# 64 short idle products for four wide ones in the head, and the last output tile's products in two halves, in a packed-attention and mixture-of-experts kernel

## The chip, the cores and the metric

The kernel runs on one core of a Trainium2 chip. The metric is the device time of one execution in microseconds (us), as the median of several runs. The engines are TensorE (PE in the profile, PEld for its weight loads), VectorE (DVE), ScalarE (ACT), GpSimd (POOL) and SyncE (SP, which issues most transfers). TensorE writes its results to PSUM, which has eight banks of 512 float32 columns on 128 partitions.

## What is computed

```python
def _attn_ref(q, k, v, p):          # q, k, v: 8 batches, 8 heads, 576 rows, 64 wide; p: 32 rows
    p_packed = sm_attn(p, k, v)     # sm_attn: softmax(scale * qq @ kk.T) @ vv
    out = sm_attn(q, p_packed, p_packed)
    return out
...
def _moe_ref(x, w_gate, w_output_gate, w1, w2):   # x: 4608 rows of 512; 8 experts, 1024 wide
    logits = x @ w_gate
    e_idx = np.argmax(logits, axis=1)
    ...
    for e in range(E):
        mask = e_idx == e
        h = np.maximum(x[mask] @ w1[e], 0.0)
        ye = h @ w2[e]
        out[mask] = gate_w[mask, None] * eom[mask, e, None] * ye
```

Two softmax attentions follow each other, the first of which packs each batch to 32 rows. Each row of the result then goes through one expert of a mixture of experts, and is scaled by its two gates.

## The kernel before, in words

The eight batches run one after another as a pipeline. Three pieces of work belong to a batch. `encode` computes the packed rows from p, k and v; `route` makes the second attention's weights and the gates; `weights` and `values_up` fetch the expert most of the batch's rows want, and fold its w1 with the packed values into G. `ffn(b)` then forms the hidden layer as products of the attention weights with G (line 674, eight chunks of 128 features), and the output as products of the hidden layer with w2. Both operands of these products are split into a high and a low part, so each chunk takes three products (`three`, line 79). The hidden layer is made for columns 0 to 255 and then for 256 to 575 of a batch (`halves`, line 603). Rows whose expert is another one are computed by `leftover`, for the first seven batches beside batch 7's work.

The order of the work is written by hand (line 939): a string START for the head, and a table PLANS for each batch, which says after which step of `ffn` which step of the other pieces is issued. Each engine's queue follows that order. PSUM banks come from two groups of four (`bank`, line 68, tags "a" and "f").

**The head.** Until TensorE has ffn work, `keep_warm(i)` (line 113) issues products of zeros whose results nobody reads. The number of them at place i is `CFG["warm"][i]`. Place 8 is called once, in batch 1's `packed_whole` (line 317), between the scores of the first and of the second half of k: at this place stand four products of 512 columns in bf16. The loop over `CFG["short"]` (line 117) belongs to place 0 and issues none, as the number is 0.

**The last tile.** `product_out` (line 701) makes one tile of 128 output rows by 512 columns: eight chunks by three products, all accumulated in one bank, with a yield after every second chunk at which the plan may put other work. The last batch takes its tiles in the order `last=(4, 2, 3)`: the remainder of 64 rows first (lines 729 to 741), then tile 2, then tile 3, which ends the kernel:

```python
            if (b, t_) == (B - 1, CFG["last"][-1]):
                rows = out[b * S + t_ * P:b * S + (t_ + 1) * P]
                right = sb.tile([P, DM // 2], F32, tag="ob", name="right", bufs=CFG["ob"])
                nc.vector.tensor_scalar_mul(ob[:, :DM // 2], ps[:, :DM // 2], sc)
                nc.scalar.activation(right, ps[:, DM // 2:], AF.Copy, scale=sc)
                nc.sync.dma_start(rows[:, :DM // 2], ob[:, :DM // 2])
                nc.sync.dma_start(rows[:, DM // 2:], right)
```

VectorE scales its left half and ScalarE its right, both from the same bank, and SyncE stores each half by a transfer of its own.

Of the kernel before, what the change touches and what calls it, by code (L numbers as in the profile page):

```python
# [10 lines left out]
F32 = mybir.dt.float32  # L11
# [3 lines left out]
AF = mybir.ActivationFunctionType  # L15
# [3 lines left out]

P = 128  # L20
BANK = 512
CFG = dict(raw=6, rq=2, pa=4, w1=2, wst=4, w2=6, a1T=2, at=2, row=2, ht=4, ob=4, up="faaf", last=(4, 2, 3), short=0, warm=(4, 1, 0, 2, 1, 1, 2, 2, 4),
           pool=("w1.0", "w1.1", "w1.2", "w1.3", "w2.0", "w2.1", "w2.2", "w2.3", "w3.3", "w4.3", "w5.3", "w6.3", "w7.3",
                 "al0.0.0"))

# [16 lines left out]
def tile_packed_attn_then_moe(ctx, tc, qT, kT, v, pT, w_go, w1, w2, kp, out):  # L42


    nc = tc.nc
    B, _, _, NPAIR, HS = qT.shape
    NG, S = v.shape[1], 2 * HS
    NP = pT.shape[3]
    E, DM, DF = w1.shape[0], out.shape[1], BANK * w1.shape[1] // 2
# [3 lines left out]
    TF = S // P  # L53
# [4 lines left out]
    FC = DF // P  # L58
# [3 lines left out]
    sb = ctx.enter_context(tc.tile_pool(name="sb", bufs=1))  # L62
    WIDE, EVEN = dict(align_bytes=512), dict(align_bytes=64)
    pool = ctx.enter_context(tc.tile_pool(name="ps", bufs=8, space=PSUM))

    NA = CFG["pa"]

    def bank(name, tag="a"):
        return pool.tile([P, BANK], F32, tag=tag, name=name, bufs=NA if tag == "a" else 8 - NA)
# [9 lines left out]
    def three(a, b):  # L79

        return [(a[i], b[j]) for i in range(len(a)) for j in range(len(b)) if i + j < 2]
# [31 lines left out]
    def keep_warm(i):  # L113

        ps = bank("warm", "a" if i == 5 else "f")
        if i == 0:
            for _ in range(CFG["short"]):
                nc.tensor.matmul(ps[:MQ, :MQ], idle[:, :MQ], idle[:, :MQ], start=True, stop=True)
        for _ in range(CFG["warm"][i]):
            if i == 1:  # L120
                for n in range(1):
                    nc.tensor.matmul(ps[:, n * P:(n + 1) * P], blank, blank, start=True, stop=True)
            else:
                nc.tensor.matmul(ps.rearrange("p (a n) -> p a n", a=2), idle[:, :P], wide_idle, start=True, stop=True)

    keep_warm(0)
    first = const.tile([P, 1], F32, name="first")
    ones = const.tile([P, P], F32R, name="ones")
# [14 lines left out]
    no_row = float(2 * B * S)  # L143
    key_i = sb.tile([P, B * T * Q * E], I32, tag="hT", name="key_i", bufs=CFG["ht"], **WIDE)
    nc.gpsimd.iota(key_i, pattern=[[1, B * T * Q * E]], base=int(big_id), channel_multiplier=0)
# [11 lines left out]
    row = const.tile([P, B, T], F32, name="row")  # L157
# [16 lines left out]
    def eng(what, *at):  # L174
        return nc.gpsimd if what + ".".join(map(str, at)) in CFG["pool"] else nc.vector

# [7 lines left out]
    def fetch(x):  # L184
# [5 lines left out]
        tag = "rq" if x == "q" else "raw"  # L190
        bufs = CFG[tag]
        if x == "v":
# [40 lines left out]
    def packed_by_parts(b, pt, nm2, sm, rs, ppc):  # L233
# [5 lines left out]
        for i, n in enumerate(PARTS):  # L239
            if i:  # L240
                keep_warm(5)
            ps = [bank("ps_s1", "f")[:, :n] for _ in range(NG)]
            by_head(ps, pt, pairs("k", b, i))
            s1.append(ps)
# [64 lines left out]
    def packed_whole(b, pt, nm2, sm, rs, ppc):  # L309
# [3 lines left out]
        if b == 1:  # L313
            for g in range(NG):
                nc.scalar.copy(a1[:, g, 0], s1[0][g])
            s1[0] = [a1[:, g, 0] for g in range(NG)]
            keep_warm(8)
# [329 lines left out]
    def ffn(b):  # L647
        ah, al = A.pop(b)
        for (t0, t1) in halves:
# [4 lines left out]
            for fc in range(FC):  # L654
# [29 lines left out]
                if not (b == c0 == fc == 0):  # L684
                    yield
            outs = [product_out(b, t_, c0, hs) for t_ in (CFG["last"] if last else range(t0, t1))]
            if b == 0 and not last:
                yield from chain.from_iterable(zip(*outs))
# [3 lines left out]
    keep = []  # L692

    def store():

        while keep:
            b, t_, ob, ps, sc = keep.pop(0)
            nc.scalar.activation(ob, ob if b < 2 and t_ < 2 else ps, AF.Copy, scale=sc)  # L698
            nc.sync.dma_start(out[b * S + t_ * P:b * S + (t_ + 1) * P], ob)

    def product_out(b, t_, c0, hs):
        w2s = W[b][1]
        r = min(P, S - t_ * P)
        ps = bank("ps_o", "f")
        c = t_ * P - c0
        ob = sb.tile([P, DM], F32, tag="ob", name="ob", bufs=CFG["ob"])
        sc = scm_all[:r, b, t_:t_ + 1]
        if t_ < TF:
            lo = 640 - 2 * P + c
            for fc in range(FC):  # L710
                for i, (a, m) in enumerate(three((hs[fc][:, c:c + P], hs[fc][:, lo:lo + P]), w2s[fc])):
                    nc.tensor.matmul(ps, a, m, start=fc == i == 0, stop=fc == FC - 1 and i == 2)  # L712
                if fc % 2 and (fc < FC - 1):
                    yield
            if (b, t_) == (B - 1, CFG["last"][-1]):
                rows = out[b * S + t_ * P:b * S + (t_ + 1) * P]
                right = sb.tile([P, DM // 2], F32, tag="ob", name="right", bufs=CFG["ob"])
                nc.vector.tensor_scalar_mul(ob[:, :DM // 2], ps[:, :DM // 2], sc)
                nc.scalar.activation(right, ps[:, DM // 2:], AF.Copy, scale=sc)
                nc.sync.dma_start(rows[:, :DM // 2], ob[:, :DM // 2])  # L720
                nc.sync.dma_start(rows[:, DM // 2:], right)
            else:
                keep.append((b, t_, ob, ps, sc))
                if b > 1 or t_ > 1:
                    store()
                else:
                    nc.scalar.copy(ob, ps)
        else:
            seq = []
            for fc in range(FC):  # L730
                wh, wl = w2s[fc]
                seq += [(hs[fc][:, c:c + 2 * r], w) for w in (wh, wl)]
            for i, (a, m) in enumerate(seq):
                nc.tensor.matmul(ps, a, m, start=i == 0, stop=i == len(seq) - 1)  # L734
                if i % 6 == 5:
                    yield
            low = sb.tile([r, DM], F32, tag="ob", name="low", bufs=CFG["ob"])
            nc.scalar.copy(low, ps[r:2 * r])
            nc.vector.tensor_tensor(ob[:r], ps[:r], low, ALU.add)
            nc.vector.tensor_scalar_mul(ob[:r], ob[:r], sc)  # L740
            nc.sync.dma_start(out[b * S + SF:(b + 1) * S], ob[:r])
        yield
# [201 lines left out]
    for b in range(B):  # L944
        plan = {}
        for x in PLANS[b].split():
            i, what = x.split(":")
# [71 lines left out]
```

## Time and profile before

| | us |
|---|---|
| median of 3 runs | 397.39 (396.75 to 397.51) |
| the profiled execution, its own time | 397.62 |
| its span, first to last instruction | 396.0 |
| TensorE busy | 386.6 (98%) |
| VectorE, ScalarE, GpSimd busy | 280.9, 182.4, 38.2 |

The profile is of one execution, whose own time stands beside its span; 1.6 us lie around the span. A product's time in it is its latency from start to end. Products overlap in the array, so a row that merges n of them lasts n - 1 times their distance plus one latency. The chain of waits is followed back from the last instruction, and gives at each step what the step waited for.

### The profile page before, as it was taken

How to read it: one execution, taken by the hardware profiler on the slowest of the kernel's cores; microseconds unless marked ns; L12 is line 12 of the kernel's file. 1: busy time of each engine (PE TensorE's matmuls, PEld its weight loads, DVE VectorE, ACT ScalarE, POOL GpSimd, SP SyncE). 2: the span in 40 equal slices, each digit the busy share in tenths (PEclk: the TensorE clock that was granted, in tenths of full speed). 3: DMA queues.
4: the chain of work that ended last, by engine and by line, in shares of the span. 5: the costliest groups of instructions: out<-in, count | busy, mean ns of one | idle time of the engine just before them, and what ended most of it. 6: DMA issues, size and time to landing. Idle time of an engine off the chain costs nothing.

```text
span 396.0 us, 9464 instructions
## 1 busy us (share of the span) xinstructions
PE 386.6 (98%) x3631; PEld 313.6 (79%) x3631; DVE 280.9 (71%) x798; ACT 182.4 (46%) x407; POOL 38.2 (10%) x40
## 2 busy tenths in 40 slices
PE   6899999999999999999999999999999999999995
PEld 2478886879779888787979888788887889798984
DVE  3789699588965967478755886659774796848820
ACT  4375437724645354533816237442645345441401
POOL 3100003410053000200002000020002000020010
PEclk9999999999999999999999999999999999999999
DMA  8999269918961399205990099602951059105911
GB/s 294 362 377 409 86 199 412 376 41 293 409 233 38 111 361 410 88 28 195 398 374 31 11 304 409 250 28 99 362 216 36 28 177 366 44 27 166 311 30 53
DMA packets 36541, 83.59 MB, mean 211 GB/s; under 512 B 3598, under 2 KB 16144, under 8 KB 36496
## 3 DMA queue, kind: packets, MB, share of 16 engines
q1 hardware_dynamic: 36032, 81.74, 56.4%
q10 hardware_dynamic: 432, 1.25, 0.8%
q8 instruction: 29, 0.48, 0.5%
q14 instruction: 16, 0.13, 0.1%
q0 software_dynamic: 32, 0.00, 0.0%
HBM read 67.76 MB, written 15.27 MB: 210 GB/s over the span
## 4 chain that ended last, share of the span: by engine, by line
PE 92%; DMA 4%; DVE 1%; issue 1%; SPq 1%; ACT 1%; POOL 0%; DVEq 0%
PE ps_o L712 44%; PE ps_h L85 26%; PE ps_o L734 7%; PE ps_G L92 4%; DMA w<-in_w_dram 3%; PE ps_s L92 2%; PE ps_pp L92 2%; PE ps_s2T L92 2%; PE ps_a1T L340 2%; PE ps_lg L92 1%; DMA kp<-in_kp_dram 1%; PE ps_h L662 1%; PE ps_lo L840 0%; PE ps_lh L840 0%; PE ps_ppT L375 0%
## 5 line engine op out<-in xcount | busy, mean ns | idle before, releaser
L712 PE MATMUL ps_o<-w2h,hT 128*128 128x512 f32 x512 | 165.3, 395 | 0.0
L712 PEld LDWEIGHTS ps_o<-w2h,hT 128*128 128x128 f32 x512 | 96.3, 188 | 23.1 <-issue 1.3
L712 PE MATMUL ps_o<-w2l,hT 128*128 128x512 f32 x256 | 99.9, 390 | 0.0
L681 DVE SCALAR_TENSOR_TENSOR hT<-ps_h,hT 128x256 fp32r<-128x256 f32 x192 | 60.6, 350 | 49.7 <-ACT hT L678 48.8
L85 PE MATMUL ps_h<-ah,Gh 128*128 128x320 f32 (+1 forms) x252 | 76.5, 303 | 0.0
L85 PE MATMUL ps_h<-ah,Gl 128*128 128x320 f32 (+1 forms) x252 | 74.6, 296 | 0.0
L85 PE MATMUL ps_h<-al,Gh 128*128 128x320 f32 (+1 forms) x252 | 74.5, 296 | 0.0
L678 ACT ACTIVATE hT<-ps_h 128x320 fp32r<-128x320 f32 (+1 forms) x128 | 51.4, 414 | 40.9 <-PE ps_h L85 38.7
L597 POOL TENSOR_TENSOR w2l<-wst,w2h 128x1024 fp32r<-128x1024 f32 x13 | 31.8, 2445 | 297.4 <-ACT w2h L594 268.3
L712 PEld LDWEIGHTS ps_o<-w2l,hT 128*128 128x128 f32 x256 | 48.1, 188 | 9.1
L85 PEld LDWEIGHTS ps_h<-ah,Gh 128*128 128x128 f32 x252 | 47.8, 190 | 3.4 <-ACT ah L486 0.8
L85 PEld LDWEIGHTS ps_h<-al,Gh 128*128 128x128 f32 x252 | 47.8, 190 | 0.4
L85 PEld LDWEIGHTS ps_h<-ah,Gl 128*128 128x128 f32 x252 | 47.8, 190 | 0.0
L594 ACT CAST w2h<-wst 128x1024 fp32r<-128x1024 f32 (+1 forms) x33 | 33.5, 1056 | 1.4 <-DMA wst<-in_w_dram 0.7
L698 ACT ACTIVATE ob<-ps_o,scm_all 128x512 f32<-128x512 f32 x27 | 18.6, 687 | 32.6 <-PE ps_o L712 27.3
L597 DVE TENSOR_TENSOR w2l<-wst,w2h 128x1024 fp32r<-128x1024 f32 (+1 forms) x20 | 23.3, 1167 | 5.5 <-ACT w2h L594 5.3
L466 ACT ACTIVATE s<-s 128x576 f32<-128x576 f32 (+2 forms) x18 | 11.4, 633 | 34.2 <-DVE s L463 34.2
L77 DVE TENSOR_TENSOR Gl<-ps_G,Gh 128x512 fp32r<-128x512 f32 x28 | 17.4, 681 | 12.9 <-ACT Gh L76 12.9
L734 PE MATMUL ps_o<-w2h,hT 128*128 128x512 f32 x64 | 25.7, 401 | 0.0
L734 PE MATMUL ps_o<-w2l,hT 128*128 128x512 f32 x64 | 25.1, 392 | 0.0
L486 ACT CAST ah<-a2T 128x576 fp32r<-128x576 f32 (+2 forms) x17 | 10.7, 639 | 26.5 <-DVE a2T L478 26.5
L92 PE MATMUL ps_G<-w,ppT 64*32 64x512 f32 (+1 forms) x288 | 16.5, 549 | 0.6 <-DMA w<-in_w_dram 0.6
(215 smaller groups left out, 425.6 us busy)
## 6 DMA issues: line engine op xcount, KB each, us to landing
w<-in_w_dram SPq DMA_DIRECT2D x36, 512.0 KB, 5.6
wst<-in_w_dram SPq DMA_DIRECT2D x36, 512.0 KB, 8.7
vt<-in_v_dram SPq DMA_DIRECT2D x15, 640.0 KB, 8.9
k<-in_kT_dram SPq DMA_DIRECT2D x14, 576.0 KB, 10.1
q<-in_qT_dram SPq DMA_DIRECT2D x14, 576.0 KB, 10.3
out_dram<-ob SPq DMA_DIRECT2D x31, 256.0 KB, 4.1
a_d<-a2T SPq DMA_DIRECT2D x16, 320.0 KB, 8.0
q<-in_qT_dram SPq DMA_DIRECT2D x4, 288.0 KB, 6.1
```

The source lines that it names most:

```text
L77: (lo_eng or nc.vector).tensor_tensor(lo, src, f(hi), ALU.subtract)
L85: res = nc.tensor.matmul(dst, a, m, start=j == 0, stop=j == len(seq) - 1)
L92: res = nc.tensor.matmul(dst, a, m, start=j == 0, stop=j == len(seqs[0]) - 1)
L466: nc.scalar.activation(sf[g], sf[g], AF.Exp, scale=QK)
L486: nc.scalar.copy(ah[:, g, ts], a2T[:, g, ts])
L594: nc.scalar.copy(h, x)
L597: eng("w", b, j).tensor_tensor(l, x, f(h), ALU.subtract)
L678: nc.scalar.activation(hT[:, :n], ps, AF.Relu)
L681: nc.vector.scalar_tensor_tensor(hT[:, d0:d0 + s1 - s0], ps[:, s0:s1], 0.0, f(hT[:, s0:s1]), op0=ALU.max, op1=ALU.subtract)
L698: nc.scalar.activation(ob, ob if b < 2 and t_ < 2 else ps, AF.Copy, scale=sc)
L712: nc.tensor.matmul(ps, a, m, start=fc == i == 0, stop=fc == FC - 1 and i == 2)
L734: nc.tensor.matmul(ps, a, m, start=i == 0, stop=i == len(seq) - 1)
```

## The change

Place 8 of the idle products gets none of the wide ones (the last number of `warm` goes from 4 to 0). The loop of short products moves from place 0 to place 8 and its number goes from 0 to 64: each is a product of 32 by 32 columns of the same zeros, with a weight load of its own, all into the first 32 rows and columns of one bank.

The last tile takes its 24 products as 48 of 256 columns: first all for the left half of the columns, in the bank as before, then all for the right half, in a second bank. VectorE scales the left half after the first 24, ScalarE the right half after the second 24. The number of yields stays at four.

```diff
-CFG = dict(raw=6, ..., last=(4, 2, 3), short=0, warm=(4, 1, 0, 2, 1, 1, 2, 2, 4),
+CFG = dict(raw=6, ..., last=(4, 2, 3), short=64, warm=(4, 1, 0, 2, 1, 1, 2, 2, 0),
...
-        if i == 0:
+        if i == 8:
             for _ in range(CFG["short"]):
                 nc.tensor.matmul(ps[:MQ, :MQ], idle[:, :MQ], idle[:, :MQ], start=True, stop=True)
...
-        if t_ < TF:
+        if (b, t_) == (B - 1, CFG["last"][-1]):
+            lo, half = 640 - 2 * P + c, DM // 2
+            rows = out[b * S + t_ * P:b * S + (t_ + 1) * P]
+            for i, to in enumerate((ps, bank("ps_o", "f"))):
+                cols = slice(i * half, i * half + half)
+                for fc in range(FC):
+                    for j, (a, m) in enumerate(three((hs[fc][:, c:c + P], hs[fc][:, lo:lo + P]), w2s[fc])):
+                        nc.tensor.matmul(to[:, :half], a, m[:, cols], start=fc == j == 0, stop=fc == FC - 1 and j == 2)
+                    if fc % (FC // 2) == FC // 2 - 1 and not (i and fc == FC - 1):
+                        yield
+                if i == 0:
+                    nc.vector.tensor_scalar_mul(ob[:, :half], to[:, :half], sc)
+                else:
+                    ob = sb.tile([P, half], F32, tag="ob", name="right", bufs=CFG["ob"])
+                    nc.scalar.activation(ob, to[:, :half], AF.Copy, scale=sc)
+                nc.sync.dma_start(rows[:, cols], ob[:, :half])
+        elif t_ < TF:
...
-            if (b, t_) == (B - 1, CFG["last"][-1]):
...
-            else:
-                keep.append((b, t_, ob, ps, sc))
```

On TensorE in the head, between the scores of batch 1's first and second half of k (ps_s), this stands before. `blank` is the tile of zeros, `warm` the bank nobody reads, and the pair of lines 124 comes four times:

```order
L92 MATMUL ps_s_344<-k,pt 32x288
L124 LDWEIGHTS blank [waits PE_49]
L124 MATMUL warm<-blank 128x512 [waits Activation_49]
...
L92 MATMUL ps_s_361<-k,pt 32x288 [waits DMAHW5_49]
L92 MATMUL ps_pg<-wgo,ppT 32x16 [waits PE_49,Activation_49]
```

And this now, with the pair of lines 118 standing 64 times:

```order
L92 MATMUL ps_s_344<-k,pt 32x288
L118 LDWEIGHTS blank [waits PE_49]
L118 MATMUL warm<-blank 32x32 [waits Activation_49]
...
L92 MATMUL ps_s_421<-k,pt 32x288 [waits DMAHW5_49]
L92 MATMUL ps_pg<-wgo,ppT 32x16 [waits PE_49,Activation_49]
```

The place and its waits are the same; only what stands between the two halves differs, and the second half still waits for its load of k.

On TensorE in the last tile, after the change (w2h and w2l are the high and low parts of w2, hT the hidden layer; rows that go on in the same pattern are left out):

```order
L715 MATMUL ps_o<-w2h,hT 128x256 [waits PE_49]
L715 MATMUL ps_o<-w2l,hT 128x256
L715 MATMUL ps_o<-w2h,hT 128x256 x2
...
L715 MATMUL ps_o<-w2h,hT 128x256 [waits DVE_49]
```

The second row with a wait is the first product of the right half, which now waits for a count of VectorE: the bank it takes is the one that the remainder tile had, and the count is that of the addition at line 739 (747 after the change). Before, the tile's 24 products of 512 columns held one wait, the first one's.

On ScalarE and SyncE at the end, from tile 2's scaling and store on (lines 698 and 699), before:

```order
L698 ACTIVATE ob<-ps_o,scm_all 128x512 [waits DMAHW2_49,PE_49,Activation_49]
L719 ACTIVATE right<-ps_o,scm_all 128x256 [waits DMAHW6_49,DMAHW3_49,DVE_49]
...
L699 DMA out_dram<-ob 128x512 [waits DMAHW4_49,Activation_49]
L720 DMA out_dram<-ob 128x256 [waits DMAHW5_49,DVE_49]
L721 DMA out_dram<-right 128x256 [waits DMAHW6_49,Activation_49]
```

And now:

```order
L698 ACTIVATE ob<-ps_o,scm_all 128x512 [waits DMAHW2_49,PE_49,Activation_49]
L722 ACTIVATE right<-ps_o,scm_all 128x256 [waits DMAHW3_49,DMAHW6_49,DVE_49,PE_49]
...
L699 DMA out_dram<-ob 128x512 [waits DMAHW4_49,Activation_49]
L723 DMA out_dram<-ob 128x256 [waits DMAHW5_49,DVE_49]
L723 DMA out_dram<-right 128x256 [waits DMAHW6_49,Activation_49]
```

ScalarE's scaling of the right half now waits for TensorE itself; its wait for VectorE is now for an earlier count, and the two stores keep their order on SyncE.

## Rows read from the trace of the kernel before

**Rows 1.** The page: span, and busy time of each engine.
```profile
span 396.0 us, 9464 instructions
PE 386.6 (98%) x3631; PEld 313.6 (79%) x3631; DVE 280.9 (71%) x798; ACT 182.4 (46%) x407; POOL 38.2 (10%) x40
```

**Rows 2.** The chain that ended last, in order of time: start us, us, what.
```profile
14.57 4.07 DMA w<-in_w_dram
...
22.64 0.72 PE ps_h L85 x6
...
300.23 5.47 PE ps_o L712 x24
...
348.50 5.75 PE ps_h L85 x48
...
380.70 11.12 PE ps_o L712 x48
391.85 0.49 DVE ob L718
392.37 0.47 ACT right L719
```

**Rows 3.** Timeline of the head: start us, us, engine, line, op, tiles, count, idle before.
```profile
1.24 1.89 PE L124 MATMUL warm<-blank 128*128 128x512 bf16 x4 [1.24 <-DVE blank L106]
...
15.39 1.04 PE L124 MATMUL warm<-blank 128*128 128x512 bf16 x4
17.25 0.72 PE L92 MATMUL ps_s<-k,pt 64*32 64x288 f32 x16 [0.82 <-DMA k<-in_kT_dram]
...
17.95 0.60 PE L124 MATMUL warm<-blank 128*128 128x512 bf16 x2
18.77 0.67 PE L92 MATMUL ps_G<-w,ppT 64*32 64x256 f32 x16 [0.22 <-DMA w<-in_w_dram]
...
19.52 0.65 ACT L633 CAST Gh<-ps_G 128x256 fp32r<-128x256 f32 x2 [0.30 <-PE ps_G L92]
19.94 0.50 PE L662 MATMUL ps_h<-ah,Gh 128*128 128x256 f32 x2
```

**Rows 4.** Timeline of the end.
```profile
379.47 0.68 DVE L739 TENSOR_TENSOR ob<-ps_o,low 64x512 f32<-64x512 f32 x1 [2.10 <-ACT low L738]
...
391.85 0.48 DVE L718 TENSOR_SCALAR ob<-ps_o,scm_all 128x256 f32<-128x256 f32 x1 [10.73 <-PE ps_o L712]
392.37 0.33 SPq L720 DMA_DIRECT2D out_dram<-ob  x1
392.37 0.47 ACT L719 ACTIVATE right<-ps_o,scm_all 128x256 f32<-128x256 f32 x1 [5.22 <-DVE ob L718]
392.87 0.33 SPq L721 DMA_DIRECT2D out_dram<-right  x1
```

**Rows 5.** DMA issues from 391 us on: count, KB each, median us to landing.
```profile
out_dram<-right SPq DMA_DIRECT2D x1, 128.0 KB, 1.7
```

**Rows 6.** Small products and loads: timeline, one tile's durations, groups by shape.
```profile
10.92 0.63 PE L92 MATMUL ps_pp<-vt,a1T 128*32 128x64 f32 x32
...
13.03 0.34 PE L85 MATMUL ps_e<-wgo,sums 128*1 128x8 f32 x8
...
L85 PEld LDWEIGHTS ps_e<-wgo,sums x8: 79/81/82, 13.0 to 13.2; 128*1 128x1 f32 x8
L85 PE MATMUL ps_e<-wgo,sums x8: 169/169/170, 13.0 to 13.2; 128*1 128x8 f32 x8
...
L92 PE MATMUL ps_pp<-vt,a1T 128*32 128x64 f32 x520 | 9.8, 220 | 0.0
...
L85 PEld LDWEIGHTS ps_h<-al,Gh 128*128 128x128 f32 x252 | 47.8, 190 | 0.4
L840 PEld LDWEIGHTS ps_lo<-wst,l_hT 128*32 128x32 f32 x64 | 1.7, 110 | 0.4 <-issue 0.4
```

**Rows 7.** Busy time of a stretch, each engine; then granted clock, DMA share, GB/s.
```profile
15.00:20.00 5.00, 3.96 (x73) 1.31 (x57) 4.24 (x13) 3.24 (x14) 0.70 (x2) 1.00 0.92 310
```

More of the change, by code (lines that the diff above doesn't have):

```diff
@@ L21 @@
 BANK = 512
-CFG = dict(raw=6, rq=2, pa=4, w1=2, wst=4, w2=6, a1T=2, at=2, row=2, ht=4, ob=4, up="faaf", last=(4, 2, 3), short=0, warm=(4, 1, 0, 2, 1, 1, 2, 2, 4),
+CFG = dict(raw=6, rq=2, pa=4, w1=2, wst=4, w2=6, a1T=2, at=2, row=2, ht=4, ob=4, up="faaf", last=(4, 2, 3), short=64, warm=(4, 1, 0, 2, 1, 1, 2, 2, 0),
            pool=("w1.0", "w1.1", "w1.2", "w1.3", "w2.0", "w2.1", "w2.2", "w2.3", "w3.3", "w4.3", "w5.3", "w6.3", "w7.3",
@@ L714, in product_out @@
                     yield
-            if (b, t_) == (B - 1, CFG["last"][-1]):
[L716 to L721, printed above, removed]
-            else:
-                keep.append((b, t_, ob, ps, sc))
-                if b > 1 or t_ > 1:
-                    store()
-                else:
-                    nc.scalar.copy(ob, ps)
+            keep.append((b, t_, ob, ps, sc))
+            if b > 1 or t_ > 1:
+                store()
+            else:
+                nc.scalar.copy(ob, ps)
         else:
```

## The prediction

> **What bounds the kernel now.** I read the page first. TensorE is busy for 98% of a span of 396.0 us [rows 1], so what counts is whether an edit makes TensorE's own stream longer or moves one of its few waits. The chain of waits in order of time then says what holds the end at the two places of the change. In the head, the chain passes through the load of the first expert's w1 (`w`, 4.07 us from 14.57 [rows 2]) into ps_G at 18.77 [rows 3]: the idle products and the second half of batch 1's scores, which run meanwhile, are beside it. At the end it is TensorE without a gap until 391.82 (380.70 + 11.12), then VectorE's scaling of the left half, then ScalarE's of the right [rows 2].
>
> The timeline of the head gives the room [rows 3]. The four wide idle products start at 15.39 and end at 16.43. TensorE then waits 0.82 us for the load of k, and starts batch 1's second score half at 17.25. The pair of idle products after it ends at 18.55, and ps_G starts at 18.77, after 0.22 us of wait for w. So the stretch from 15.39 may grow by 0.82 us unseen, and by 0.22 us more before ps_G moves. Past that a delay counts in full: ScalarE's casts of ps_G start at 19.52 just behind it, and the products at 19.94 wait for them [rows 3].
>
> The timeline of the end [rows 4] shows VectorE on the left half from 391.85 to 392.33, ScalarE on the right half from 392.37 to 392.84, idle before that because of VectorE, and SyncE issuing the two stores at 392.37 and 392.87. The second lands about 1.7 us after its issue [rows 5]; the span closes at 396.0.
>
> **The change, part by part.**
>
> *Head.* Four products of 512 columns go (1.04 us [rows 3]); 64 loads of 32 columns with products of 32x32 come, all into the same 32 rows of PSUM, at the same place of the queue. No row shows this form. One bound is the row of ps_pp with its 128x64 products: 32 of them in 0.63 us, one lasting 0.22, so (0.63 - 0.22)/31 = 13 ns apart [rows 6]; but these go to four strips of PSUM in turn. The nearest row is ps_e: eight small products into one place, each with its own load, (0.34 - 0.169)/7 = 24.4 ns apart [rows 6], although each load is listed with 81 ns and each product with 169. Loads thus overlap products even in one place of the array, and those of ps_h too (loads of 190 ns [rows 6] for products 120 ns apart, below). What ps_e lacks is width: a load of 32 columns is listed with 110 ns and its load of one column with 81 [rows 6], so 31 columns cost 29 ns. If the load's 30 ns of streaming overlap the product, the larger of 24.4 and 30 ns is the pitch; if they add, 24.4 + 29 = 53 ns, and with 24 more moving columns at 0.42 ns (512 columns in 0.22 us, from the pairs in [rows 3]) 63 ns. I take 30 ns, as ps_e, the nearest row, shows overlap, and keep 13 and 63 for the range. 64 x 30 ns = 1.92 us ends at 17.31, 0.06 us past the arrival of k; the 0.22 us before ps_G take that. Cost: **0**. If those covers were gone, it would be 0.88 us (1.92 - 1.04). At 13 ns it is 0 as well, at 63 ns 64 x 63 = 4.03, less 1.86 and 0.22: +1.95 us.
>
> The Trainium skill states a price against this edit ("TensorE: Matmul & The Clock Gate", section "Wait — 56ns, not 53.3ns?"): where instructions are decoded in firmware, some 62 ns are spent on every MATMUL. By that rule, as an estimate from the page, 64 products would take 4.0 us and the kernel some 1.9 us more than without the edit. The trace disagrees with 24.4 and 13 ns [rows 6], so the rule does not seem to hold here.
>
> Nor is there a gain to fetch. The granted clock reads 1.00 from 15 to 20 us [rows 7], and the pairs of idle products at 17.95, after the gap, are 0.22 us apart (0.60 - 0.38, the 0.38 being one product's own latency: 1.04 = 0.38 + 3 x 0.22), which is the 2.4 GHz level; the first four, at 1.24, took 1.89 us, about twice as long [rows 3]. The gap did not cost the clock before, so filling it gives nothing back.
>
> *Last tile, products.* 24 products of 512 columns become 48 of 256, with 24 more weight loads. The chain has both kinds in steady state: 24 wide ones of ps_o take 5.47 us, 48 of 256 columns of ps_h take 5.75 [rows 2], which is 228 and 120 ns each, with the same 128x128 loads hidden behind the same operand type. Cost: **+0.28 us**, on the path. A lower bound is 0, as half the columns cannot take less than half the time; an upper bound comes if a load of 190 ns were exposed in every pair: 48 x 190 ns = 9.1 us, +3.65; the 120 ns of ps_h, with the same loads, speak against it, so I leave that end out.
>
> *Last tile, what follows.* The left half is complete after 24 of the 48 products, some 2.9 us before the end. VectorE's 0.48 us and the left store's issue now lie beside the right half's products. On the path stays ScalarE's 0.47 us [rows 4], which no longer queues behind VectorE, then the same store of 128 KB. What goes is 392.37 - 391.85 = 0.52 us. **-0.52 us**, if ScalarE starts as soon behind TensorE as VectorE does now (391.82 to 391.85 [rows 2]); bounds are -0.4 and -0.6 us, as a start may take a tenth more or the store may gain one. SyncE's queue has nothing between the stores, so the left one cannot hold up the right one.
>
> The new wait is that of the right half's first product on a count of VectorE. It is for the last reader of the bank it takes: the remainder tile's sum at line 739, done at 380.15 [rows 4], six microseconds before the last tile starts. It costs nothing.
>
> **Sum.** 0 + 0.28 - 0.52 = -0.24 us. The profiled execution took 397.62 us, of which 396.0 are the span, so 397.38 by its own time; the median of the runs is 0.23 below that execution, and the forecast for it 397.39 - 0.24 = **397.15 us**. About 0.2%, or 0.8 us, is the least that a measurement of this kernel can tell from no change, so I expect none that can be told.
>
> **The rivals.**
>
> *The short products outlast the wait (slower).* The place is 15.39 to 17.25. If load and product add in the one strip of the array, the pitch p is 53 to 63 ns and everything behind ps_G moves by 64p - 2.08 us. It decides from 32.5 ns on, and with the end's gain it is over 0.2% from (2.08 + 0.24 + 0.79)/64 = 49 ns on. At 53 ns it gives 397.15 + 1.31 = 398.5, at 63 ns 399.1. For it: no row has this form, all 64 have the same target, and the forecast leaves only 2.5 ns. Against: ps_e at 24.4 ns. Chance 0.12. The skill's 62 ns rule would give the same sum.
>
> *The clock falls.* A product of 32x32 uses a small part of the array, and TensorE may be granted 1.2 GHz during or after them. Then the work from 18.77 to about 22.6 (3.87 us on the chain, ps_G to the first products at line 85 [rows 2, 3]) takes up to twice as long: about +3 us, 400.1. Against: the small products of ps_e at 13.03 [rows 6] were followed by idle products at the full level at 15.39 [rows 3]. Chance 0.03.
>
> *The right half's wait is in truth for VectorE's scaling of the left half (the change does not do what it says).* Then TensorE stops for about 0.5 us between the halves: 397.65, still within 0.2%. The order speaks against it. Chance 0.04.
>
> *More than expected comes back (faster).* The right store, alone on the queues, lands sooner and the head's start shifts by luck; it takes 0.55 us beyond the sum to 396.6, for which I see no source but 1.7 us of landing. Chance 0.04.
>
> **How the numbers follow.** The forecast itself has 0.77, of which pitches from 32.5 to 49 ns are the upper part; its own range is 396.8 to 397.9. For 8 in 10, I add the spread of the three runs (396.75 to 397.51) below and part of the first rival above: 396.7 to 398.4. Within 0.2%: 0.77 + 0.04 = 0.81; slower: 0.12 + 0.03 = 0.15; faster 0.04.
>
> **What would show it.** The 64 products should end near 17.3 and ps_G should start at 18.8; ps_G later than 19.0 proves the first rival, idle pairs over 0.3 us apart the second. The last tile should take 5.75 us in place of 5.47, VectorE's scaling end some 2.4 us before ScalarE's starts, and ScalarE start within 0.05 us of the last product. The prediction is wrong if ps_G moves by a microsecond, if the halves are more than 130 ns apart, or if the end after the last product shrinks by less than 0.4 us.

## The result, and the profile after

The changed kernel takes 399.19 us (median of 5 runs, 399.01 to 400.75) against 397.39 before (5 runs, 396.75 to 397.54): 1.0056 times as long, with a 95% interval of 1.0042 to 1.0070. It is slower by 1.8 us where 397.15 was forecast, and lies outside the range of 396.7 to 398.4.

The profiled execution took 399.1 us. The page, to be held against [rows 1]: 84 products more on TensorE and 1.5 us more span.

```profile
span 397.5 us, 9633 instructions
PE 388.2 (98%) x3715; PEld 317.1 (80%) x3715; DVE 281.3 (71%) x798; ACT 182.5 (46%) x407; POOL 38.2 (10%) x40
```

The timeline of the changed kernel's head answers to [rows 3] (start us, us, engine, line, op, tiles, count, idle before):

```profile
16.30 0.89 PE L118 MATMUL warm<-blank 128*32 128x32 bf16 x29
17.49 1.03 PE L118 MATMUL warm<-blank 128*32 128x32 bf16 x35 [0.30 <-issue]
18.45 0.71 PE L92 MATMUL ps_s<-k,pt 64*32 64x288 f32 x16
...
19.68 0.66 PE L92 MATMUL ps_G<-w,ppT 64*32 64x256 f32 x16
```

The short products stand (0.89 - 0.176)/28 = 25.5 ns apart, 0.176 being one's latency, close to the 30 ns of the forecast. There is a pause of 0.30 us after the first 29, in which TensorE waits for nothing that the profile shows. The head is 0.91 us later than in the profile of before, but it is so already at the first short product (16.30 against 15.39), and ps_G is 0.91 late too. In this execution the short products cost ps_G nothing beyond that.

The last tile in the chain of waits, and then the timeline of the end; they answer to [rows 2, 4]:

```profile
386.62 5.76 PE ps_o L715 x48
```

```profile
389.53 0.48 DVE L719 TENSOR_SCALAR ob<-ps_o,scm_all 128x256 f32<-128x256 f32 x1 [8.16 <-PE ps_o L715]
...
390.04 0.33 SPq L723 DMA_DIRECT2D out_dram<-ob  x1
...
392.41 0.47 ACT L722 ACTIVATE right<-ps_o,scm_all 128x256 f32<-128x256 f32 x1 [5.01 <-PE ps_o L715]
392.91 0.33 SPq L723 DMA_DIRECT2D out_dram<-right  x1
```

The 48 products take 5.76 us, the forecast's 5.75. VectorE is done 2.4 us before ScalarE starts, and ScalarE starts right behind the last product. ScalarE's scaling ends at 392.88, within 0.04 us of before (392.84). Up to here the kernel is as fast as it was. But the span now ends 4.62 us behind the scaling (397.5 - 392.88), where it ended 3.16 behind it (396.0 - 392.84). **All of the profiled execution's 1.5 us lies behind the last instruction of any compute engine.**

The DMA view of that stretch shows why. Before, from 393 to 396 us, it has packets of one queue only, those of the data (queue, kind: packets, MB, share of 16 engines):

```profile
q1 hardware_dynamic: 288, 0.26, 25.0%
```

After the change, from 393 to 396.2 us, there are two queues (the last line is the store's issue: count, KB, median us to landing):

```profile
q1 hardware_dynamic: 144, 0.13, 12.5%
q8 instruction: 1, 0.02, 2.5%
...
out_dram<-right SPq DMA_DIRECT2D x1, 128.0 KB, 3.2
```

The second queue carries the program's instructions, and one packet of it is there, a fetch of 0.02 MB. Its 2.5% of 16 engines over 3.2 us are 1.3 us of one DMA engine. The last store lands 3.2 us after its issue, not 1.7 as in [rows 5]. Three narrower stretches, 393.4 to 393.8, 393.8 to 394.2 and 394.8 to 395.8, show the order:

```profile
q8 instruction: 1, 0.02, 19.8%
q1 hardware_dynamic: 13, 0.01, 9.1%
```

```profile
q1 hardware_dynamic: 121, 0.11, 78.7%
```

```profile
q1 hardware_dynamic: 9, 0.01, 4.7%
```

The fetch starts first, at 393.7. The store's packets follow; 135 of the 144 have started by 394.3, and the other 9 only from 394.9 on, when the fetch has run its 1.3 us. So 9 packets, a sixteenth of the store, appear to stand behind it on one engine (the profile does not name the engine of a packet), and the end of the program waits for them. The page of before counts 29 packets of the instruction queue, that of the changed kernel 30:

```profile
q8 instruction: 29, 0.48, 0.5%
```

```profile
q8 instruction: 30, 0.49, 0.5%
```

The instruction queue's traffic fits TensorE: 0.49 MB for 7430 recorded products and loads is 66 bytes each. The last packet starts 1.3 us behind the end of the last product (392.37).

### The profile page after: what moved, and what is told of

Read it like the earlier page. It is cut to its first block, busy times and chain, and to the rows that moved or that the text cites. A ratio compares the mean times of both kernels' runs of the same rounds, so it can differ in the third digit from the quotient of the medians.

```text
span 397.5 us, 9633 instructions
## 1 busy us (share of the span) xinstructions
PE 388.2 (98%) x3715; PEld 317.1 (80%) x3715; DVE 281.3 (71%) x798; ACT 182.5 (46%) x407; POOL 38.2 (10%) x40
## 4 chain that ended last, share of the span: by engine, by line
PE 97%; DMA 1%; DVE 0%; issue 0%; ACT 0%
PE ps_o L728 43%; PE ps_h L85 26%; PE ps_o L742 7%; PE ps_G L92 4%; PE ps_pp L92 3%; PE ps_s L92 3%; PE ps_s2T L92 2%; PE ps_a1T L340 2%; PE ps_o L715 1%; PE ps_lg L92 1%; DMA kp<-in_kp_dram 1%; PE ps_a1T L257 1%; PE ps_h L662 1%; PE ps_lh L848 0%; PE ps_lo L848 0%; PE warm L118 0%
## 5 line engine op out<-in xcount | busy, mean ns | idle before, releaser
L728 PE MATMUL ps_o<-w2h,hT 128*128 128x512 f32 x496 | 160.3, 395 | 0.0
L728 PEld LDWEIGHTS ps_o<-w2h,hT 128*128 128x128 f32 x496 | 93.3, 188 | 22.4 <-issue 1.3
L728 PE MATMUL ps_o<-w2l,hT 128*128 128x512 f32 x248 | 96.8, 390 | 0.0
L728 PEld LDWEIGHTS ps_o<-w2l,hT 128*128 128x128 f32 x248 | 46.6, 188 | 8.9 <-DVE w2l L597 0.2
L742 PE MATMUL ps_o<-w2h,hT 128*128 128x512 f32 x64 | 25.7, 401 | 0.0
L742 PE MATMUL ps_o<-w2l,hT 128*128 128x512 f32 x64 | 25.0, 391 | 0.0
```

## The experiments

Theory F: the change makes TensorE's program longer, by 168 instructions (60 products net in the head and 24 in the tail, each with a load). That puts the fetch of one more block behind the last product, where it delays the last store. Rival H: the short products, or the clock around them, cost the time. Rival S: the halves cost it.

All kernels below are compared with runs of the kernel before on the same chip. "Tail" is the span's end less the end of ScalarE's last scaling, in the profiled execution.

**Each edit alone, and padding alone.** The first is the kernel before with the head's part of the change alone:

```diff
-short=0, warm=(4, 1, 0, 2, 1, 1, 2, 2, 4)
+short=64, warm=(4, 1, 0, 2, 1, 1, 2, 2, 0)
...
-        if i == 0:
+        if i == 8:
```

> The kernel before with the 64 short products at place 8, the last tile as before: 120 TensorE instructions more than before. Theory F (an instruction fetch of 16 KB, put off to the end by the longer program, holds up the last store): the time depends only on whether a fetch falls behind the last product; either 397.4 (none) or about 398.9 with a landing of over 3 us of the last store. Rival H (the short products or the clock around them cost): 399.2 with ps_G about 0.9 us later. Rival S (the halves cost): 397.4.

Measured: 399.02 us, 1.0037 (1.0022 to 1.0052). Tail 4.36 us. Its DMA view from 392 us on has the fetch, which starts at 393.1, and two late stores:

```profile
q8 instruction: 1, 0.02, 1.5%
...
out_dram<-ob SPq DMA_DIRECT2D x1, 128.0 KB, 3.0
out_dram<-right SPq DMA_DIRECT2D x1, 128.0 KB, 2.8
```

In this execution TensorE ends its last product at 391.81, against 391.82 in that of the kernel before: its 1.2 us of longer span (397.2 against 396.0) are the tail's.

The second takes the numbers of the idle products back in the changed kernel, so that only the halves are left:

```diff
-short=64, warm=(4, 1, 0, 2, 1, 1, 2, 2, 0)
+short=0, warm=(4, 1, 0, 2, 1, 1, 2, 2, 4)
```

> The kernel before with the last tile in two halves, the four wide idle products kept: 48 TensorE instructions more than before. Theory F: with so few the last fetch should stay ahead of the last store, 397.15 (the sum of +0.28 and -0.52), last store landing in 1.7 us. Rival H: 397.15. Rival S: 399.2.

Measured: 396.82 us, 0.9988 (0.9978 to 0.9998). Tail 3.10 us, landing 1.7.

S falls: the halves alone are not slower. The head edit alone has the fetch and the late stores, but for the medians H is not yet excluded. The next kernel has neither edit; to `before`, behind the wide products of place 0, it adds

```diff
+        if i == 0:
+            for _ in range(84):
+                nc.tensor.matmul(ps[:MQ, :MQ], idle[:, :MQ], idle[:, :MQ], start=True, stop=True)
```

> The kernel before, neither edit, with 84 short products of zeros at place 0: 168 TensorE instructions more than before, as many as the change adds. Theory F: a fetch behind the last product, the last stores landing some 1.5 us later, 398.9. Rivals H and S: 397.4.

Measured: 399.47 us, 1.0055 (1.0038 to 1.0072), the changed kernel's ratio but for a hundredth of a per cent. Its DMA view from 392 us on:

```profile
q8 instruction: 1, 0.02, 1.8%
...
out_dram<-ob SPq DMA_DIRECT2D x1, 128.0 KB, 3.3
out_dram<-right SPq DMA_DIRECT2D x1, 128.0 KB, 3.1
```

Both stores are late, tail 4.61 us. Program length alone brings the 1.5 us of the end, with the old head at place 8 and the old last tile. Its head also waits elsewhere, 0.69 us for v and 0.65 for p, so not all of its 2.1 us is the end's: in the profiled execution the scaling ends 0.25 us later than before (393.09 against 392.84).

**Too much padding.** The same loop with another count, added to the changed kernel:

```diff
+            for _ in range(64):
```

> The changed kernel with 64 more short products of zeros at place 0, where TensorE waits 2.2 us for its first data: 296 TensorE instructions more than before, or one block of 256 and 40. Theory F: the fetch moves away from the last store, 397.15 and a landing of 1.7 us. Rivals H and S: 399.2, as nothing of the head at place 8 or of the last tile is different from the changed kernel.

Measured: 401.61 us, 1.0092 (1.0060 to 1.0123), and 397.9 to 403.2 over ten runs. My number is a miss, but the end is as F has it: the last fetch starts at 389.7, the store lands in 1.7 us, tail 3.18. In the one profiled execution (401.28 us) the loss moved to the head; why the ten runs lie so far apart is not shown. TensorE's timeline there, and then the engines' busy times with the granted clock (the number behind POOL's) from 15 to 20 us:

```profile
12.66 0.71 PE L92 MATMUL ps_s2T<-q,ppT 64*32 64x288 f32 x16
15.80 1.22 PE L92 MATMUL ps_s2T<-q,ppT 64*32 64x288 f32 x16 [2.43 <-issue]
```

```profile
15.00:20.00 5.00, 4.20 (x86) 2.35 (x87) 1.84 (x7) 2.14 (x9) 0.00 (x0) 0.50 0.97 362
```

TensorE stops for 2.43 us in the middle of a run of products, waiting for nothing that the profile shows. An instruction packet starts at 13.26, while the DMA engines are nearly full (a share of 0.97 from 15 to 20 us). After this halt the granted clock is 0.50, which is 1.2 GHz, and 16 products that took 0.71 us take 1.22. The 0.30 us pause in the changed kernel is of the same kind by its marks: a packet starts at 14.95, and the products go on at 17.49, 2.54 us later in both.

The place of the pause in the program says more. The head edit alone, with 64 short products or with 52, the changed kernel and two variants of it below all pause 0.21 to 0.31 us in front of the 30th short product, and the padded kernel halts among products of other work (ps_s2T). Yet in all six TensorE has by then started 220 weight loads and 219 products (220 in the padded one). So the pause belongs to a place counted from the program's start, and not to the products that stand there. In the padded kernel TensorE had already reached this place when the packet started; in the changed kernel it had 55 products still to do. In all six the products go on 2.4 to 2.5 us after the packet's start. The length of the pause then depends on how early the packet comes.

**Fewer instructions.** With 48 instructions added, once as 24 short products at place 0 of the kernel before (the edit is against the kernel with 84), once as 28 short products at place 8 (against the head edit alone):

```diff
-            for _ in range(84):
+            for _ in range(24):
```

> The kernel before with 24 short products of zeros at place 0: 48 TensorE instructions more than before, as many as the halves alone add. Theory F (a fetch of 16 KB of TensorE's instructions stands behind the last product once the program has grown past some boundary between 48 and 120 instructions, and the last stores queue behind it): no fetch after the last product, both last stores landing in 1.7 us, 397.3. Rival P (added products at place 0 cost time by themselves, through the clock or the first loads): like the 84, some 2 us more, in proportion 0.6 us, 397.9 or more.

Measured: 396.98 us, 0.9994 (0.9982 to 1.0006). Tail 3.11, landing 1.7 for both stores.

```diff
-short=64
+short=28
```

> The kernel before with 28 in place of 64 short products at place 8, the last tile as before: 48 TensorE instructions more than before, and 28 x 25 ns = 0.7 us of products where 1.04 us stood. Theory F: no fetch behind the last product, stores landing in 1.7 us, 397.3. Rival H (replacing the wide products by short ones costs by itself, through the clock): some 399, with the stores landing in 1.7 us.

Measured: 396.94 us, 0.9994 (0.9979 to 1.0009). Tail 3.12, landing 1.7. So P falls at this size, and H in the form that short products cost the clock: the granted clock is 1.00 from 10 to 30 us with all 64 of them too, in the changed kernel and in the head edit alone.

**The store taken away.** To tell the store's delay from TensorE's own wait for its instructions:

```diff
-                nc.sync.dma_start(rows[:, cols], ob[:, :half])
+                if i == 0:
+                    nc.sync.dma_start(rows[:, cols], ob[:, :half])
```

> The changed kernel without the store of the last tile's right half, so those 128 x 256 values are not written. Theory F1 (the store is what is late, as part of it queues behind the fetch on one DMA engine): nothing is left to be late, and the span ends some 2.5 us sooner behind the last scaling than in the changed kernel (4.6 us from the end of ScalarE's scaling to the end of the span there), about as soon as in the next kernel. Rival F2 (TensorE itself waits for its last instructions, and the store is late beside that): the span still ends some 3 us or more behind the scaling, over 1 us later than in the next kernel.

> The halves alone with the four wide idle products kept, and without the store of the last tile's right half, so those 128 x 256 values are not written. There is no fetch behind the last product here, so this is the measure for the kernel ahead: the span should end some 1.5 us behind ScalarE's scaling under either theory.

Measured: from the end of scaling to the end of the span 2.45 us with the fetch (it starts at 393.2) and 2.34 without it. The absolute 1.5 of the second expectation was too low, but the comparison speaks for F1: with the fetch the end is 0.1 us later where no store stands behind it, and 1.5 where one does. F2, which asked for over 1 us, falls, as far as one run of each can tell.

**Both edits, below and near the boundary.** The changed kernel with fewer short products, 16 and then 28:

```diff
-short=64
+short=16
```

> Both edits, with 16 in place of 64 short products: 72 TensorE instructions more than before. Theory F: the boundary lies between 48 and 120 instructions more. If it is above 72, no fetch stands behind the last product, the last store lands in 1.7 us, and both edits together take 396.9 (the sum of -0.24 on 397.1); if below, 398.3 or more with a landing of 3 us. Rival H (short products at place 8 beside the halves cost by themselves): over 398 with a landing of 1.7 us.

Measured: 396.85 us, 0.9993 (0.9981 to 1.0005). Tail 3.11, no fetch behind the last product.

```diff
-short=64
+short=28
```

> Both edits, with 28 in place of 64 short products: 96 TensorE instructions more than before. The same two outcomes as at 16: 396.9 with a landing of 1.7 us where no fetch stands behind the last product, 398.3 or more with a landing of 3 us where one does; theory F allows no other pairing of time and landing. If 16 has the fetch, 28 has it too.

Measured: 397.24 us, 0.9996 (0.9986 to 1.0006). Here the fetch comes, but at 395.8, after the store has landed, and costs next to nothing, tail 3.28:

```profile
q8 instruction: 1, 0.02, 2.0%
...
out_dram<-right SPq DMA_DIRECT2D x1, 128.0 KB, 1.7
```

**An attempt at mending it.** 44 more short products behind the last tile's last product:

```diff
                 nc.sync.dma_start(rows[:, cols], ob[:, :half])
+            ps = bank("warm")
+            for _ in range(44):
+                nc.tensor.matmul(ps[:MQ, :MQ], idle[:, :MQ], idle[:, :MQ], start=True, stop=True)
```

> The changed kernel, all of it, with 44 more short products of zeros behind the last tile's last product, where TensorE has nothing left to do: 256 TensorE instructions more than before, one whole block, so that the end of the program stands in its block as it did before the change. Theory F: the fetch that stood behind the last product moves to before it, the last store lands in 1.7 us, and adding work makes the changed kernel faster: 397.2, or up to 397.7 if the 64 products in the head have a price of their own of some 0.5 us. Rivals H and S: 399.2, as the head and the halves are those of the changed kernel.

Measured: 400.48 us, 1.0075 (1.0055 to 1.0096), landing 3.2, tail 4.79: a miss. The fetch stays behind the last product, at 393.5. So the rule I used, that the end is safe again after one whole block, is wrong. One reading is that blocks are counted from the program's start, as the pause in the head suggests, and nothing ahead of the last product has changed; no run tests it for the end. That the time did not fall with the fetch still there agrees with the late store as the cause, but proves nothing new, and of the 0.8 us over the changed kernel the tail has only 0.2.

**The head's own price.** As every kernel with 64 short products had either that fetch or a stall, one with 52 and the old last tile, 24 instructions shorter than the head edit alone (the edit is against that):

```diff
-short=64
+short=52
```

> The kernel before with 52 short products at place 8, the last tile as before: 96 TensorE instructions more than before, 24 fewer than with 64 of them. Theory F: as with both edits and 28 products, which also adds 96, no fetch stands before the last stores' landing, they land in 1.7 us, and the time is 397.2 to 397.6. Rival H (the short products have a price of their own, some 25 ns each of which is not covered): 12 products of the 64 gone, so at most 0.3 us less than the 399.02 of the 64, 398.7.

Measured: 397.83 us, 1.0013 (1.0001 to 1.0025). The fetch comes at 395.5, behind the landings, tail 3.35. This misses both numbers and is nearer to F's: by the ratios 12 short products less are worth 1.0 us (0.0024 x 397), of which 0.3 can be the products. Of the head edit's 1.5 us (0.0037 x 397), then, up to 0.5 may be its own (0.0013 x 397), of which 0.2 lies in the tail. That 0.5 is not shown: the kernel of the next paragraph gave ratios 0.0015 apart on two occasions, more than the 0.0013 here.

**The halves again.** The second kernel of this section, built once more.

> The halves alone once more, with more rounds, as the candidate for a version that beats both kernels: 396.8 to 397.1, landing 1.7 us, no fetch behind the last product. Theory F and the sum of the prediction give the same here (-0.24 us); if the kernel is no faster than before at all, the gain of the halves is below what can be measured.

Measured: 397.30 us, 1.0003 (0.9994 to 1.0012). With 0.9988 the first time, the gain of the halves is not above what can be told, and two such ratios of one kernel can differ by more than their intervals say. I have no version that is clearly faster than the kernel before; both edits with 16 short products are as fast as it.

The instructions added and the tail, over all kernels that write the whole output (start of the last fetch in us):

| instructions more than before | last fetch | landing of the right store, us | tail, us |
|---|---|---|---|
| 0, 48 (four runs of three kernels), 72 | 379.9 to 384.8, before the last product is done | 1.7 | 3.10 to 3.16 |
| 96 (two kernels) | 395.5, 395.8, after the stores | 1.7 | 3.28, 3.35 |
| 120, 168 (two kernels), 256 | 393.1 to 393.7, ahead of the right store | 2.8 to 3.2 | 4.36 to 4.79 |
| 296 | 389.7, during tile 2, the last but one | 1.7 | 3.18 |

## Why the prediction was wrong

- **Last tile, products: right.** +0.28 forecast, 5.76 us against 5.47 measured, +0.29.
- **Last tile, what follows: wrong, and this is the step that failed.** VectorE's 0.52 us did leave the path, as written. What failed is "then the same store of 128 KB", with the 1.7 us of [rows 5]. The store landed in 3.2 us. I counted every added instruction by what it takes on TensorE and never by its place in the program, which is fetched in packets of 0.02 MB over the DMA engines that carry the data too. The sum for the profiled execution is then -0.24 + 1.5 in place of -0.24. The sign that I had named for it came out: the end behind the last product was to shrink by at least 0.4 us, and it grew by 0.95 (397.5 - 392.37 against 396.0 - 391.82).
- **Head: the pitch was nearly right, the cover was not a constant.** 25.5 ns measured against 30 taken. The waits of [rows 3], 0.82 us for k and 0.22 for w, belong to one execution. In the execution of the halves alone, the wide idle products of place 8 start at 15.91 and end without any wait for k, and ps_G starts at 18.54; in that of the head edit alone the short ones start at the same 15.91, and ps_G starts at 19.22, 0.68 us later. Pauses for instructions within the burst (0.2 to 0.3 us) were not in the sum at all. How much of this reaches the end is not shown. With 64 short products at place 8 and place 0 as before, tile 2's scaling near the end starts at 386.3 to 386.7 in four profiled executions; in seven with at most 28 it starts at 385.4 to 386.8. "0" should have been a range, from 0 to some 0.7.
- **The rivals.** The first gave 398.5 to 399.1 and so came within 0.1 us of the time by luck, by a mechanism that did not occur: its pitch of 53 to 63 ns was 25.5. Its sign, ps_G later than 19.0, did come (19.68), but because the whole head was 0.91 us late in that execution, so the sign was badly chosen. The 62 ns per MATMUL that the Trainium skill gives for decoding in firmware ("TensorE: Matmul & The Clock Gate", section "Wait — 56ns, not 53.3ns?") are not seen in this burst either: 25.5 ns. The clock did not fall in the changed kernel (the granted clock is 1.00 from 10 to 30 us), but fell in the kernel with more padding, behind a halt. The right half's first product did not wait. No rival named the fetch, and so the chance of 0.15 for slower was too low.
- **The total.** For the profiled execution: +0.25 us up to the last tile, by ScalarE's scaling of tile 2 (386.71 against 386.46), +0.29 for the halves, -0.5 for the scaling, +1.46 for the tail, together 1.5. For the medians: 1.2 to 1.5 for the fetch, 0 to 0.5 for the head, and -0.2 or nothing for the halves, against 1.8 measured.

What stays open: which instruction sets the last fetch off. Behind the last product lie a branch over a loop and the exit of the program. They may be why the last fetch comes near 393 us with some lengths and near 395.5 with others, but the runs do not show the rule. Whether the head edit has a price of its own, by pauses or by lost cover, is open too.

## What to carry to other kernels

Count added instructions as program bytes as well as time: TensorE's program comes in packets of some 16 KB (0.49 MB in 30 packets here) over the DMA engines that also carry the data. In these runs a fetch in front of the last store made the tail 1.2 to 1.6 us longer, and one that came late in the crowded head stopped TensorE for 0.2 to 2.4 us, whatever the added instructions did. To tell such a cost from an edit's own, pad the unchanged kernel with as many idle instructions in a free place, and look at the instruction queue and the landing of the last store. A wait seen in one profile is not a cover to spend: look whether it is there in other executions first.

## What was not expected of the hardware

- One instruction packet took 1.2 to 1.4 us of one DMA engine, and a store of 128 KB landed 1.1 to 1.6 us later when the packet came just ahead of its own 144 (2.8 to 3.3 us against 1.7 in the other kernels).
- TensorE paused 0.21 to 0.31 us, and in one kernel 2.43 us, always after the same 220 weight loads, with 2.4 to 2.5 us between the start of an instruction packet in a stretch of crowded DMA engines and the next product.
- Products of 32x32 into one place of the array, each with its own load of 32 columns, stood 25.5 ns apart, nearly as close as ps_e's with loads of one column (24.4).
